# Recurrent attention and routed experts on one core: two products moved to GpSimd, the first expert's weights staged in two buffers, the slot table read through another queue

## The chip, the cores and the metric

The kernel runs on one core of a Trainium2 chip. The metric is device microseconds (us) of that core for one execution, lower is better. Engines are PE (TensorE), DVE (VectorE), ACT (ScalarE), POOL (GpSimd) and SP (SyncE, which here only issues DMAs); PEld is PE's loading of weights.

## What is computed

Two stages, the second fed by the first. The first is a recurrence over 768 steps for 4 x 8 heads of width 40; its output, laid out as 3072 tokens of 320 numbers, goes to one of 8 experts each:

```python
for t in range(S):                                   # 768 steps, state [4, 8, 40, 40]
    y[:, :, t] = einsum('bhd,bhde->bhe', rt, state)
    Sa = einsum('bhde,bhe->bhd', state, at)
    state = state * wt[:, :, None, :] - einsum('bhd,bhe->bhde', Sa, bt) + einsum('bhd,bhe->bhde', vt, kt)
x = y.transpose(0, 2, 1, 3).reshape(3072, 320)
logits = x @ w_gate                                  # 8 experts
e_idx = argmax(logits, axis=1)
gate_w = softmax(logits)[arange(N), e_idx]
eom = sigmoid(x @ w_output_gate)
for e in range(8):                                   # w1[e] 320 x 1024, w2[e] 1024 x 320
    mask = e_idx == e
    out[mask] = gate_w[mask, None] * eom[mask, e, None] * (maximum(x[mask] @ w1[e], 0) @ w2[e])
```

## The kernel before

**Attention.** The 768 steps are cut into 12 chunks `c` of 64. Within a chunk the recurrence becomes triangular systems, so that PE can work on it. Each chunk goes through four generators:

- `scan(c)` (L98) loads the decays `w` (L104) and `a`, `k`, `b` as one tile `D` (L106) through SP, and makes the running products `P` and `I` on DVE (L111 to L118).
- `prep(c)` (L126) makes what only the inputs need. `Av` is `a` times `I` and `a` times `P`, one product for columns 0 to 32 (L173) and one for 33 to 63 (L174), both on DVE. SP copies pieces of `Av` into `Am` (L180) and into `LA` (L167). DVE makes `KBt` (L190). PE multiplies `KBt` by `Am` (L203), ACT copies the result into `N` (L214) and `LA` (L216), and GpSimd zeroes the triangle of `LA` (an affine select, L218). GpSimd also clears parts of `LA` and `N` (L136, L144).
- `tinv` (L227) inverts the small triangles of two chunks at a time by products and sums on DVE (L290 and L295 are among them).
- `crit(c, q)` and `tail(c, q)` solve and finish a chunk in two units, q = 0 and 1, eight heads on each half of the partitions. `crit` applies `Tc` and `N` on PE (L368) with ACT's copies `As` between (L359, three in a unit); each copy waits for PE and PE for each copy. GpSimd's product `Dt` (L385) scales the state for the next chunk. `tail` transposes (L430), makes `M` (PE L440, DVE L444), `pY` (L455, L456), and DVE writes the result `x` (L458).

For each unit `route` stores `x` to a DRAM tensor `xd` (SP, L616), transposes it (L619) and computes the gate's logits (L623). After chunks 3, 7, 10 and 11, `pick` (L633) gives each token a slot of its expert, and GpSimd scatters 128 records of 16 bytes at a time into the table `tab` in DRAM (L695): eight scatters after chunk 3, eight after chunk 7, six and two after the last ones.

**Experts.** Each takes the tokens of its slots in groups of 120 columns times up to four. Weights are split into a high part (ACT cast) and the rest (DVE subtract), and each product is made of three (L776, L789 to L791), so PE runs nearly full there.

**What overlaps.** `run` (L473) steps through the units. At each step of `crit` it advances a background generator by four steps (`RATE`): preparation and inversion of later chunks, and, when the last of these is done, `early` (L809). That one stages the weights of expert 0 (`weights`, L708) in six blocks: SP load (L719, L722 or L729), ACT cast (L723, L730), DVE subtract (L725, L731), all through one buffer `st` (pool `sp0`, one buffer). Then, when the tokens of the first eight chunks have slots (`HALF`, L609) and 30 more steps are gone, `slots` (L798) reads the table into `tr` on SP (L802) and makes the index tiles on DVE (L804, L806). `tokens` (L734) gathers two groups of rows from `xd` on GpSimd (L745) and transposes them (L753), and the first four products of expert 0 follow (L776).

Each engine executes its own list in order. The lists are made by the tile framework's scheduler, which orders what the program issues by dependences and its own estimates; `issue_after(mark)` holds an instruction behind another one in the order. `mark['x']` is the last load of `XS` (L338), `mark['y']` the last `pY` product (L456). A tile's load can't begin before the last reader of the same buffer is done.

The lines that set where the weights and the table come:

```python
        with s.tc.tile_pool(name="sp0", bufs=1, side="right") as sp:
            w = s.weights(0, s.wpa, sp)
            s.W0 = next(w)
            yield from w
...
        for _ in range(30):
            yield
        with s.tc.issue_after(mark['x']):
            s.tabs = s.slots(s.tp0)
```

Of the kernel before, what the change touches and what calls it, by code (L numbers as in the profile page):

```python
# [9 lines left out]
F32 = mybir.dt.float32  # L10
# [4 lines left out]
AF = mybir.ActivationFunctionType  # L15
# [39 lines left out]
class Att:  # L55
# [70 lines left out]
    def prep(s, c):  # L126
# [45 lines left out]
        with s.tc.issue_after(s.mark['r', 0]) if c == 1 else ExitStack():  # L172
            V.tensor_tensor(out=Av[:, :, 0:33], in0=a[:, :, 0:33], in1=I[:, :, 1, ::-1], op=ALU.mult)  # L173
            V.tensor_tensor(out=Av[:, :, 33:64], in0=a[:, :, 33:64], in1=P[:, :, 0, 1:32], op=ALU.mult)  # L174
        with s.tc.issue_after(s.mark['n', 0]) if c == 1 else ExitStack():
# [167 lines left out]
    def crit(s, c, q):  # L343
# [13 lines left out]
        def move(h):  # L357
            x = s.p2.tile([128, 8, 40], F32, name="As", tag="As", bufs=2)
            nc.scalar.activation(out=x, in_=pa, func=AF.Copy, scale=s.hq[:, h:h + 1])  # L359
            return x  # L360
# [57 lines left out]
    def tail(s, c, q, sink):  # L418
# [38 lines left out]
        x = s.p2.tile([128, 8, 40], F32, name="x", bufs=2)  # L457
        nc.vector.tensor_tensor(out=x, in0=pY[:, :, 0:40], in1=WT[:, 8 * q:8 * q + 8], op=ALU.mult)  # L458
        s.post.append(sink(c, q, x))
# [98 lines left out]
class Moe:  # L558
# [148 lines left out]

    def weights(s, e, wp, sp):  # L708

        nc = s.nc  # L710
        w1h = wp.tile([128, 3, FF], F32R, name="w1h", tag="w1h")
        w1l = wp.tile([128, 2, FF], F32R, name="w1l", tag="w1l")
        w2h = wp.tile([128, 8, DM], F32R, name="w2h", tag="w2h")
        w2l = wp.tile([128, 8, DM], F32R, name="w2l", tag="w2l")
        yield w1h, w1l, w2h, w2l
        for k in range(3):
            st = sp.tile([128, FF], F32, name="st", tag="st")
            if k < 2:
                nc.sync.dma_start(out=st, in_=s.w1[e, 128 * k:128 * k + 128])  # L719
            else:  # L720
                for h in range(2):
                    nc.sync.dma_start(out=st[64 * h:64 * h + 64], in_=s.w1[e, 256:320])  # L722
            nc.scalar.copy(out=w1h[:, k], in_=st)  # L723
            l, r = (w1l[:, k], slice(0, 128)) if k < 2 else (w1h[64:128, 2], slice(64, 128))
            nc.vector.tensor_tensor(out=l, in0=st[r], in1=w1h[r, k].bitcast(F32), op=ALU.subtract)  # L725
            yield
        for k, n in ((0, 3), (3, 3), (6, 2)):
            st = sp.tile([128, FF], F32, name="st", tag="st")[:, 0:n * DM].rearrange("p (k f) -> p k f", k=n)
            nc.sync.dma_start(out=st, in_=s.w2[e, 128 * k:128 * (k + n)].rearrange("(k p) f -> p k f", p=128))  # L729
            nc.scalar.copy(out=w2h[:, k:k + n], in_=st)  # L730
            nc.vector.tensor_tensor(out=w2l[:, k:k + n], in0=st, in1=w2h[:, k:k + n].bitcast(F32), op=ALU.subtract)  # L731
            yield

# [63 lines left out]

    def slots(s, pool):  # L798

        nc = s.nc  # L800
        tr = pool.tile([TS, 32, 4], F32, name="tr", tag="tr")
        nc.sync.dma_start(out=tr, in_=s.tab.rearrange("(t p) f -> p t f", p=TS))  # L802
        tb = pool.tile([TS, 4, 32], F32, name="tb", tag="tb")
# [5 lines left out]
    def early(s, ctx, psx, mark):  # L809

        pool = lambda n, b: ctx.enter_context(s.tc.tile_pool(name=n, bufs=b, side="right"))
        s.wpa, s.tp0 = pool("wpa", 1), pool("tp0", 1)
        with s.tc.tile_pool(name="sp0", bufs=1, side="right") as sp:
            w = s.weights(0, s.wpa, sp)
            s.W0 = next(w)
            yield from w
        while not s.half:
            yield
        for _ in range(30):
            yield  # L820
        with s.tc.issue_after(mark['x']):
            s.tabs = s.slots(s.tp0)
        t = s.tokens(s.tabs, 0, 0, 2, s.tp0, psx)
# [242 lines left out]
```

## Time and profile before

| | |
|---|---|
| three runs | 726.17, 728.7, 730.5 us; median 728.7 |
| profiled execution | 729.31 us |
| span of its profile | 727.6 us |
| mean granted clock of PE | 0.947 of full |
| PE busy | 650.8 us (89% of the span), 8898 matmuls |
| PEld busy | 581.6 us (80%) |
| DVE busy | 470.3 us (65%) |
| ACT busy | 339.2 us (47%) |
| POOL busy | 206.5 us (28%) |
| DMA | 85.12 MB, mean 117 GB/s |

The span runs from the first to the last record of the execution that the profiler took. Some 1.7 us lie around it. Busy times of engines overlap. A "group" of the profile is all instructions of one line, engine and tile names, with their count, busy time and mean; behind it stands how long the engine was idle just before them, and what ended that. A row of the timeline has start and duration in us, engine, line, operation, output and inputs, shape, count, and in brackets an idle time of the engine ahead of it with what ended it ("<-DVE As L381"). The last `x` of attention is made at 467.6 us. The experts' products fill PE from 473 us to the end.

### The profile page before, as it was taken

The numbers are of one execution on the slowest core, as the hardware profiler recorded it, in microseconds if no ns is written. First come the engines' busy times: TensorE is split into PE (matmuls) and PEld (weight loads), VectorE is DVE, ScalarE is ACT, GpSimd is POOL, SyncE is SP. The second block draws the span as 40 slices with busy tenths as digits, with TensorE's granted clock in tenths as the row PEclk, the third lists the DMA queues.
The fourth block names the chain that finished last, engine by engine and source line by source line (L and its number), as shares of the span: only waits on it lengthen the run. The fifth ranks groups of instructions, "written<-read, shape, count | busy, mean of one in ns | idle before, by whom it ended". The sixth has DMA issues, their size and how long they took to land.

```text
span 727.6 us, 21192 instructions
## 1 busy us (share of the span) xinstructions
PE 650.8 (89%) x8898; PEld 581.6 (80%) x8898; DVE 470.3 (65%) x914; ACT 339.2 (47%) x781; POOL 206.5 (28%) x316
## 2 busy tenths in 40 slices
PE   6768997898999899899998699779999999999994
PEld 5556876787987788788887588679999998898994
DVE  6678689868986899897796254353575445554230
ACT  2567662674377368437632244142464334433120
POOL 8442220340233247222122100325533231402111
PEclk9867898999999999999999799999999999999998
DMA  7864653266337637632234551075475533431000
GB/s 165 190 150 128 155 143 79 76 152 160 99 111 180 133 79 178 156 92 86 76 76 88 115 141 50 20 184 174 114 240 147 166 117 104 153 109 34 18 13 28
DMA packets 64387, 85.12 MB, mean 117 GB/s; under 512 B 34586, under 2 KB 51613, under 8 KB 62846
## 3 DMA queue, kind: packets, MB, share of 16 engines
q1 hardware_dynamic: 60446, 74.79, 40.4%
q0 software_dynamic: 3840, 8.91, 4.3%
q8 instruction: 72, 1.18, 0.7%
q14 instruction: 29, 0.24, 0.1%
HBM read 67.59 MB, written 8.96 MB: 105 GB/s over the span
## 4 chain that ended last, share of the span: by engine, by line
PE 59%; DVE 12%; DMA 12%; ACT 7%; issue 5%; POOL 2%; SPq 1%; POOLq 0%; ACTq 0%; DVEq 0%
PE ph L776 14%; PE pa L368 5%; PE po L791 5%; DMA D<-in_din_dram 5%; PE po L789 5%; PE po L790 5%; PE pM L440 4%; DMA st<-in_w_dram 4%; PE pt L152 3%; PE pl L203 3%; PE pS L406 3%; PE pY L456 2%; ACT N L214 2%; PE pY L455 2%; PE pa L355 2%
## 5 line engine op out<-in xcount | busy, mean ns | idle before, releaser
L218 POOL TENSOR_SCALAR_AFFINE_SELECT LA<-LA 64x192 f32<-64x192 f32 x144 | 60.7, 451 | 85.9 <-ACT LA L216 79.4
L781 DVE SCALAR_TENSOR_TENSOR hl<-ph,hh 128x480 fp32r<-128x480 f32 (+1 forms) x76 | 41.8, 562 | 66.4 <-ACT hh L780 60.3
L789 PE MATMUL po<-w2h,hh 128*120 128x320 f32 x256 | 79.2, 313 | 3.6 <-ACT hh L780 3.5
L776 PE MATMUL ph<-xh,w1h 128*128 128x480 f32 (+1 forms) x228 | 79.4, 353 | 2.0 <-DVE hl L781 1.3
L776 PE MATMUL ph<-xl,w1h 128*128 128x480 f32 (+1 forms) x228 | 78.8, 348 | 0.0
L790 PE MATMUL po<-w2l,hh 128*120 128x320 f32 x256 | 78.0, 308 | 0.0
L780 ACT ACTIVATE hh<-ph 128x480 fp32r<-128x480 f32 (+1 forms) x76 | 36.8, 497 | 87.1 <-PE ph L776 79.9
L791 PE MATMUL po<-w2h,hl 128*120 128x320 f32 x256 | 75.8, 310 | 0.0
L794 POOL DMA_INDIRECT out_dram<-y,ti x32 | 33.5, 1047 | 137.5 <-DVE y L793 78.1
L359 ACT ACTIVATE As<-pa,hq 128x320 f32<-128x320 f32 x80 | 42.0, 527 | 55.7 <-PE pa L368 46.8
L203 PE MATMUL pl<-Am,KBt 120*128 120x192 f32 (+1 forms) x288 | 59.1, 337 | 9.5 <-ACT LA L216 6.0
L368 PE MATMUL pa<-As,Tc 64*32 64x40 f32 x1792 | 52.9, 208 | 16.0 <-ACT As L359 13.0
L214 ACT ACTIVATE N<-pl 32x192 f32<-32x192 f32 (+1 forms) x138 | 51.6, 374 | 25.8 <-PE pl L203 12.0
L368 PEld LDWEIGHTS pa<-As,Tc 64*32 64x32 f32 x1792 | 41.8, 114 | 26.9 <-ACT As L359 14.6
L456 PE MATMUL pY<-KB,M 128*64 128x64 f32 (+1 forms) x768 | 54.7, 230 | 7.0 <-DVE M L444 6.9
L695 POOL DMA_INDIRECT tab<-rec,si x24 | 24.8, 1033 | 114.5 <-DVE rec L692 47.8
L203 PEld LDWEIGHTS pl<-Am,KBt 120*128 120x128 f32 x288 | 44.6, 197 | 14.9 <-ACT LA L216 8.9
L456 PEld LDWEIGHTS pY<-KB,M 128*64 128x64 f32 x768 | 48.3, 143 | 9.8 <-DVE M L444 7.6
L455 PE MATMUL pY<-Sd,R 128*64 128x64 f32 (+1 forms) x704 | 55.7, 233 | 0.3 <-DVE base L669 0.3
L776 PE MATMUL ph<-xh,w1l 128*128 128x480 f32 (+1 forms) x152 | 52.9, 348 | 0.0
L440 PE MATMUL pM<-R,VU 128*128 128x128 f32 x384 | 51.0, 283 | 1.5 <-ACT VU L432 1.4
L789 PEld LDWEIGHTS po<-w2h,hh 128*120 128x120 f32 x256 | 46.3, 182 | 5.8 <-ACT hh L780 4.6
(186 smaller groups left out, 1564.5 us busy)
## 6 DMA issues: line engine op xcount, KB each, us to landing
D<-in_din_dram SPq DMA_DIRECT2D x12, 1080.0 KB
st<-in_w_dram SPq DMA_DIRECT2D x16, 512.0 KB
st<-in_w_dram SPq DMA_DIRECT2D x16, 480.0 KB
XS<-in_vt_dram SPq DMA_DIRECT2D x24, 256.0 KB
XU<-in_vt_dram SPq DMA_DIRECT2D x24, 256.0 KB
VU<-in_vl_dram SPq DMA_DIRECT2D x24, 208.0 KB
w<-in_win_dram SPq DMA_DIRECT2D x12, 371.2 KB
st<-in_w_dram SPq DMA_DIRECT2D x16, 256.0 KB
```

The source lines that it names most:

```text
L203: nc.tensor.matmul(pl[:, i, 0:nj], KBt[:, 6 * side + g0 + i].rearrange("p n t -> p (n t)"), Am[:, g0 + i:g0 + i + 6 * nj - 5:6, 0:64], sta ...
L214: s.mark['n', c] = nc.scalar.activation(out=nn, in_=pn, func=AF.Copy, scale=-1.0).ins
L218: g.affine_select(out=la[:, :, i], in_=la[:, :, i], pattern=[[0, nj], [1, C]], base=0, channel_multiplier=-1, compare_op=ALU.is_gt, fill=0.0)
L359: nc.scalar.activation(out=x, in_=pa, func=AF.Copy, scale=s.hq[:, h:h + 1])
L368: nc.tensor.matmul(pa[o + w:o + w + 32, i], m(p)[o:o + 64], x[o:o + 64, i, :], start=start, stop=True, tile_position=(o, o + w), skip_grou ...
L440: nc.tensor.matmul(pM[:, i], VU[:, h0 + i].rearrange("p n t -> p (n t)"), R[:, :, h0 + i], start=True, stop=True)
L455: nc.tensor.matmul(o, R[:, side, i, :], Sf[:, 40 * i:40 * i + w], start=True, stop=False)
L456: s.mark['y'] = nc.tensor.matmul(o, Ms[i // 4][:, i % 4, side, :], Kf[:, k:k + w], start=not c, stop=True).ins
L776: nc.tensor.matmul(ph, l, r, start=(i == 0), stop=(i == 7))
L789: nc.tensor.matmul(po, hh[f][:, ts_], w2h[:, f], start=(f == 0), stop=False)
L790: nc.tensor.matmul(po, hh[f][:, ts_], w2l[:, f], start=False, stop=False)
L791: nc.tensor.matmul(po, hl[f][:, ts_], w2h[:, f], start=False, stop=(f == 7))
```

## The change

1. From chunk 2 on, the two products of `Av` are issued on GpSimd (`g`) and no longer on DVE. Chunks 0 and 1 stay on DVE.
2. `weights` gets a second form, used for expert 0 only (`lag` 12). Pool `sp0` has two buffers. There are eight steps: step k issues the load of block k and the cast and subtract of block k - 2, with 12 yields behind each step. All of a step is ordered behind the last load of `XS` (`mark['x']`), the last `As` copy (`mark['as']`) and the last `x` (`mark['ds']`) that the program has issued by then.
3. `slots` reads the table through GpSimd's queue (now line 826), behind `mark['ds']` in place of `mark['x']`.

Lines below 716 keep their numbers. In the new kernel the weight loads are L720, L723 and L727, the casts L732 and L737, the subtracts L734 and L738, the gathers L769, the transposes of gathered rows L777, the first products L800.

```diff
         with s.tc.issue_after(s.mark['r', 0]) if c == 1 else ExitStack():
-            V.tensor_tensor(out=Av[:, :, 0:33], in0=a[:, :, 0:33], in1=I[:, :, 1, ::-1], op=ALU.mult)
-            V.tensor_tensor(out=Av[:, :, 33:64], in0=a[:, :, 33:64], in1=P[:, :, 0, 1:32], op=ALU.mult)
+            (g if c > 1 else V).tensor_tensor(out=Av[:, :, 0:33], in0=a[:, :, 0:33], in1=I[:, :, 1, ::-1], op=ALU.mult)
+            (g if c > 1 else V).tensor_tensor(out=Av[:, :, 33:64], in0=a[:, :, 33:64], in1=P[:, :, 0, 1:32], op=ALU.mult)
...
-            nc.scalar.activation(out=x, in_=pa, func=AF.Copy, scale=s.hq[:, h:h + 1])
+            s.mark['as'] = nc.scalar.activation(out=x, in_=pa, func=AF.Copy, scale=s.hq[:, h:h + 1]).ins
...
-        nc.vector.tensor_tensor(out=x, in0=pY[:, :, 0:40], in1=WT[:, 8 * q:8 * q + 8], op=ALU.mult)
+        s.mark['ds'] = nc.vector.tensor_tensor(out=x, in0=pY[:, :, 0:40], in1=WT[:, 8 * q:8 * q + 8], op=ALU.mult).ins
...
-    def weights(s, e, wp, sp):
+    def weights(s, e, wp, sp, lag=0, mark=None):
...
+        def load(k):
             st = sp.tile([128, FF], F32, name="st", tag="st")
...
+            return st
+
+        def halve(k, st):
+            if k < 3:
+                nc.scalar.copy(out=w1h[:, k], in_=st)
...
+        if not lag:
+            for k in range(6):
+                halve(k, load(k))
+                yield
+            return
+        st = {}
+        for k in range(6 + 2):
+            with ExitStack() as order:
+                for m in ('x', 'as', 'ds'):
+                    if m in mark:
+                        order.enter_context(s.tc.issue_after(mark[m]))
+                if k >= 2:
+                    halve(k - 2, st[k - 2])
+                if k < 6:
+                    st[k] = load(k)
+            for _ in range(lag):
+                yield
...
-    def slots(s, pool):
+    def slots(s, pool, q=None):
...
-        nc.sync.dma_start(out=tr, in_=s.tab.rearrange("(t p) f -> p t f", p=TS))
+        (q or nc.sync).dma_start(out=tr, in_=s.tab.rearrange("(t p) f -> p t f", p=TS))
...
-        with s.tc.tile_pool(name="sp0", bufs=1, side="right") as sp:
-            w = s.weights(0, s.wpa, sp)
+        with s.tc.tile_pool(name="sp0", bufs=2, side="right") as sp:
+            w = s.weights(0, s.wpa, sp, 12, mark)
...
-        with s.tc.issue_after(mark['x']):
-            s.tabs = s.slots(s.tp0)
+        with s.tc.issue_after(mark['ds']):
+            s.tabs = s.slots(s.tp0, s.nc.gpsimd)
```

The scheduler makes all lists anew, so rows move beyond the edited lines. Three places follow; numbers behind a tile's name tell its buffers apart.

DVE before, near the end of the preparations (chunk 11). `tmpf` and `Yt` belong to the inversion, `M` to a unit that is being finished, `rbm` is a test of the range of the decays:

```order
L411 TENSOR_TENSOR XS_155<-tmS,Dt 40x8x40
L118 TENSOR_TENSOR I<-I,rq 120x792
L174 TENSOR_TENSOR Av<-D,P 120x12x31
L466 TENSOR_REDUCE rbm<-wsq 120x1
L295 TENSOR_REDUCE Yt<-tmpf 128x8x4 x2
L467 TENSOR_REDUCE rbm<-rqm 120x1
L444 TENSOR_TENSOR M<-pM,mM 128x512
L173 TENSOR_TENSOR Av<-D,I 120x12x33
```

and GpSimd after the change, the last two chunks prepared (10 and 11):

```order
L385 TENSOR_TENSOR Dt<-LA 40x32
L218 AFFINE_SELECT LA<-LA 64x3x64 x2
L174 TENSOR_TENSOR Av<-D,P 120x12x31
L218 AFFINE_SELECT LA<-LA 64x3x64 x2
L173 TENSOR_TENSOR Av<-D,I 120x12x33
L218 AFFINE_SELECT LA<-LA 64x2x64 x2
L218 AFFINE_SELECT LA<-LA 64x3x64 x4
L218 AFFINE_SELECT LA<-LA 64x2x64 x2
L136 MEMSET LA 32x2112
L174 TENSOR_TENSOR Av<-D,P 120x12x31
L173 TENSOR_TENSOR Av<-D,I 120x12x33
```

The products left DVE's list, where they stood among pieces of the inversion and of `M`. On GpSimd those of chunk 10 stand between the selects of chunk 9, and those of chunk 11 behind the clearing of `LA`.

SP's queue where the weights and the table are read, before (units of chunks 9 and 10; `R`, `VU`, `XU`, `XS` are inputs of the units to come):

```order
L334 DMA VU_140<-in_vl_dram 104x8x64
L719 DMA st<-in_w_dram 128x1024
L802 DMA tr<-tab 120x32x4
L333 DMA R_139<-in_rl_dram 40x512 x2
L616 DMA xd<-x 128x320
L339 DMA XU_152<-in_vt_dram 64x1024
L338 DMA XS_155<-in_vt_dram 64x1024
L719 DMA st<-in_w_dram 128x1024
L334 DMA VU_144<-in_vl_dram 104x8x64
L722 DMA st<-in_w_dram 64x1024 x2
```

and after:

```order
L334 DMA VU_140<-in_vl_dram 104x8x64
L338 DMA XS_155<-in_vt_dram 64x1024
L333 DMA R_139<-in_rl_dram 40x512 x2
L616 DMA xd<-x 128x320
L720 DMA st<-in_w_dram 128x1024 x2
L339 DMA XU_152<-in_vt_dram 64x1024
L334 DMA VU_144<-in_vl_dram 104x8x64
L723 DMA st<-in_w_dram 64x1024 x2
L727 DMA st<-in_w_dram 128x3x320
```

The table read is gone from SP. The first two weight loads stand together behind the store of `x` of the first unit of chunk 9; before, the first stood ahead of that store and the second three transfers behind it.

ACT at the same place, before:

```order
L399 COPY XU_152<-pa 64x8x40
L723 CAST w1h<-st 128x1024
L359 ACTIVATE As<-pa,hq 128x320
L621 COPY xT<-pxt 128x384
L434 ACTIVATE Sd<-ptS 128x320
L432 COPY VU_144<-ptU 128x8x64
L624 COPY LG<-pxt 128x16
L359 ACTIVATE As<-pa,hq 128x320
L723 CAST w1h<-st 128x1024
L359 ACTIVATE As<-pa,hq 128x320
```

and after, with the scatters and the table read on GpSimd under it:

```order
L624 COPY LG<-pxt 128x16
L359 ACTIVATE As<-pa,hq 128x320
L732 CAST w1h<-st 128x1024 x2
L359 ACTIVATE As<-pa,hq 128x320
L398 COPY XU_156<-pa 64x8x40
L399 COPY XU_156<-pa 64x8x40
L732 CAST w1h<-st 128x1024
```

```order
L695 DMA tab<-rec,si 3840x4 x4
L385 TENSOR_TENSOR Dt<-LA 40x32
L695 DMA tab<-rec,si 3840x4 x4
L826 DMA tr<-tab 120x32x4
L769 DMA xg<-xd,ti 120x320 x2
L695 DMA tab<-rec,si 3840x4 x7
```

The first two casts stood ahead of the first and of the third `As` of a unit; now both stand together ahead of the third. On GpSimd the read follows the eight scatters that it depends on, with four of them ahead of `Dt` (two before the change).

## Rows read from the trace of the kernel before

**Rows 1.** By stretch: length, busy PE, PEld, DVE, ACT, POOL, clock, DMA share, GB/s.
```profile
45.00:365.00 320.00, 292.30 (x5390) 252.66 (x5391) 262.56 (x533) 194.44 (x495) 92.59 (x174) 0.95 0.50 124
395.00:435.00 40.00, 29.57 (x566) 26.00 (x562) 13.40 (x22) 12.92 (x25) 4.18 (x4) 0.83 0.55 128
```

**Rows 2.** Groups by line, the `Av` products: busy, mean ns | idle before, releasers.
```profile
L173 DVE TENSOR_TENSOR Av<-D,I 120x396 f32<-120x396 f32 x12 | 6.8, 568 | 6.6 <-DMA w<-in_win_dram 4.4 <-DMA xd<-x 2.0
L174 DVE TENSOR_TENSOR Av<-D,P 120x372 f32<-120x372 f32 x12 | 6.5, 546 | 13.0 <-DMA D<-in_din_dram 9.9 <-DMA VU<-in_vl_dram 1.7 <-DMA R<-in_rl_dram 1.4
```

**Rows 3.** Timeline of DVE, one wait for `D` in chunk 11.
```profile
307.63 0.55 DVE L174 TENSOR_TENSOR Av<-D,P 120x372 f32<-120x372 f32 x1 [2.61 <-DMA D<-in_din_dram]
```

**Rows 4.** Timeline of PE, five gaps that end with a DVE result.
```profile
54.70 1.01 PE L368 MATMUL pa<-As,Tc 64*32 64x40 f32 x24 [2.03 <-DVE As L381]
...
112.09 0.69 PE L619 MATMUL pxt<-ident,x 128*128 128x128 f32 x2 [1.33 <-DVE w L103]
...
178.88 0.55 PE L619 MATMUL pxt<-ident,x 128*128 128x128 f32 x3 [1.83 <-DVE x L458]
...
245.45 0.27 PE L456 MATMUL pY<-KB,M 128*64 128x64 f32 x1 [0.80 <-DVE M L444]
...
309.50 0.37 PE L456 MATMUL pY<-KB,M 128*64 128x64 f32 x1 [2.99 <-DVE M L444]
```

**Rows 5.** Busy time in the half-clock stretches behind those gaps: one, and the sum.
```profile
309.10:312.50 3.40, 3.00 (x60) 2.90 (x60) 3.40 (x12) 0.00 (x0) 0.00 (x0) 0.50 0.08 25
...
sum 20.50, PE 17.61 PEld 15.65 DVE 18.07 ACT 6.97 POOL 1.25; mean PE 4.40 PEld 3.91 DVE 4.52 ACT 1.74 POOL 0.31
```

**Rows 6.** GpSimd's selects (min/median/max ns) and timeline rows of three engines.
```profile
L218 POOL TENSOR_SCALAR_AFFINE_SELECT LA<-LA x144: 292/355/4680, 27.3 to 353.4; 64x192 f32<-64x192 f32 x96, 64x128 f32<-64x128 f32 x48
...
273.83 8.97 POOL L218 TENSOR_SCALAR_AFFINE_SELECT LA<-LA 64x192 f32<-64x192 f32 x8 [1.86 <-ACT As L359]
...
333.86 0.68 DVE L290 TENSOR_TENSOR tmpf<-Tt,Yt 128x512 f32<-128x512 f32 x1
...
335.06 0.83 DVE L290 TENSOR_TENSOR tmpf<-Tt,Yt 128x512 f32<-128x512 f32 x1
...
225.94 0.54 DVE L174 TENSOR_TENSOR Av<-D,P 120x372 f32<-120x372 f32 x1
...
233.79 1.41 PE L203 MATMUL pl<-Am,KBt 120*128 120x192 f32 x7 [0.43 <-ACT WT L154]
```

**Rows 7.** Timeline of SP's queue: the table read and the second weight load.
```profile
402.34 0.36 SPq L802 DMA_DIRECT2D tr<-tab  x1
...
407.32 0.53 SPq L719 DMA_DIRECT2D st<-in_w_dram  x1
```

**Rows 8.** Timeline of ACT and PE around those loads.
```profile
414.04 1.04 ACT L723 CAST w1h<-st 128x1024 fp32r<-128x1024 f32 x1 [10.26 <-DMA st<-in_w_dram]
...
400.65 0.55 PE L368 MATMUL pa<-As,Tc 64*32 64x40 f32 x20 [3.48 <-ACT As L359]
...
415.57 1.28 PE L368 MATMUL pa<-As,Tc 64*32 64x40 f32 x32 [6.30 <-ACT As L359]
```

**Rows 9.** Half-clock stretches from 401.3 (3.4 us) and 411.5 (10.3 us), summed.
```profile
sum 13.70, PE 9.63 PEld 8.58 DVE 3.12 ACT 4.42 POOL 0.00; mean PE 4.81 PEld 4.29 DVE 1.56 ACT 2.21 POOL 0.00
```

**Rows 10.** Timeline: two results `x`; two weight loads issued together, the second one's cast.
```profile
386.04 0.49 DVE L458 TENSOR_TENSOR x<-pY,WT 128x320 f32<-128x320 f32 x1 [0.60 <-PE pS L406]
...
395.40 0.49 DVE L458 TENSOR_TENSOR x<-pY,WT 128x320 f32<-128x320 f32 x1 [1.51 <-PE pY L456]
...
474.49 0.81 SPq L719 DMA_DIRECT2D st<-in_w_dram  x2
...
482.77 1.04 ACT L723 CAST w1h<-st 128x1024 fp32r<-128x1024 f32 x1 [1.81 <-DMA st<-in_w_dram]
```

**Rows 11.** The scatters as a group; the table read in the chain of waits.
```profile
L695 POOL DMA_INDIRECT tab<-rec,si x24 | 24.8, 1033 | 114.5 <-DVE rec L692 47.8 <-DMA tab<-rec,si 43.1 <-DVE M L444 20.1
...
402.34 4.26 DMA tr<-tab
```

More of the change, by code (lines that the diff above doesn't have):

```diff
@@ L715, in weights @@
         yield w1h, w1l, w2h, w2l
-        for k in range(3):
+        def load(k):
             st = sp.tile([128, FF], F32, name="st", tag="st")
@@ L719, in weights @@
                 nc.sync.dma_start(out=st, in_=s.w1[e, 128 * k:128 * k + 128])
-            else:
+            elif k == 2:
                 for h in range(2):
                     nc.sync.dma_start(out=st[64 * h:64 * h + 64], in_=s.w1[e, 256:320])
[L723 to L732, printed above, removed]
+            else:
+                k, n = ((0, 3), (3, 3), (6, 2))[k - 3]
+                st = st[:, 0:n * DM].rearrange("p (k f) -> p k f", k=n)
+                nc.sync.dma_start(out=st, in_=s.w2[e, 128 * k:128 * (k + n)].rearrange("(k p) f -> p k f", p=128))
@@ new lines, in load @@
+            return st
+        def halve(k, st):
+            if k < 3:
+                nc.scalar.copy(out=w1h[:, k], in_=st)
+                l, r = (w1l[:, k], slice(0, 128)) if k < 2 else (w1h[64:128, 2], slice(64, 128))
+                nc.vector.tensor_tensor(out=l, in0=st[r], in1=w1h[r, k].bitcast(F32), op=ALU.subtract)
+            else:
+                k, n = ((0, 3), (3, 3), (6, 2))[k - 3]
+                nc.scalar.copy(out=w2h[:, k:k + n], in_=st)
+                nc.vector.tensor_tensor(out=w2l[:, k:k + n], in0=st, in1=w2h[:, k:k + n].bitcast(F32), op=ALU.subtract)
```

## The prediction, made before the changed kernel ran

> **What bounds the kernel now.** I read the busy time by stretch first [rows 1], to see which engine is full where. From 45 to 365 us, where chunks are prepared while earlier chunks are solved, PE is busy 292.3 of 320 us and DVE 262.6: two nearly full engines that feed each other. From 395 to 435 us PE has only 29.6 us of work in 40, and a granted clock of 0.83. These are the two places that the change touches.
>
> For the first place the groups by line show the two products that make `Av` [rows 2]: 12 each, 568 and 546 ns, and before them 6.6 and 13.0 us in which DVE stood still, mostly for the load of `D`. The timeline of DVE shows one such wait [rows 3]: 2.61 us ahead of the product of chunk 11. DVE works in order, so whatever PE needs from it next comes late. PE's timeline has five gaps that end with a DVE result shortly after such a wait [rows 4]: 2.03, 1.33, 1.83, 0.80 and 2.99 us, 8.98 in all. Four of the five are followed by stretches in which the granted clock is half (1.2 GHz in place of 2.4). These last 20.5 us, and PE is busy 17.61 of them [rows 5]; at full clock that work would take half, so they cost up to 8.8 us.
>
> For the second place I read SP, ACT and PE together [rows 7, 8]. SP's queue issues the read of the slot table at 402.34 us, when the last scatter has landed. Everything behind it waits, the second weight load too, which goes out at 407.32. ACT has that load's cast in its order ahead of an `As` copy, waits 10.26 us for the data, and PE waits 6.30 us for the copy. The first load did the same a little earlier, for 3.48 us of PE. Two half-clock stretches follow, with 9.63 us of PE work in them [rows 9].
>
> **The change, part by part.** *The products move.* Ten chunks (2 to 11) take 10 x (0.568 + 0.546) = 11.1 us of work and most of the 19.6 us of waiting [rows 2] off DVE. I count the 11.1 us as nothing in themselves: PE is the fuller engine, and what it waits for DVE is in the gaps. Of the 8.98 us of gaps I take three quarters, 6.7, because some would wait for the next thing (the `M` product, an `As` copy); of the clock, two thirds of 8.8, 5.9. Bounds: 0, where the waits only change their name, and all of both.
>
> The waits for `D` now stand in GpSimd's queue. Behind them are the selects on `LA` of the chunk before, the clearing of `LA`, and `Dt`; a chunk prepared here is solved two chunks later, so 4 us are covered. `Av` itself may come later: in chunk 8 it ends at 226.5 and PE's first product with it starts at 233.79 [rows 6], 7.3 us later, with the copies into `Am` between. SP's queue has the copies of `Av` too, with loads of the next units behind them; a delay of 1 or 2 us is covered by their buffers (three of `XS` and `XU`).
>
> What does a product cost on GpSimd? No row has one. From below: DVE's own 0.55 us [rows 2]. From above: 4.7 us, since a select of 192 columns, 355 ns at the median, took 4680 ns in the worst case and eight of them 8.97 us [rows 6], in a stretch where DVE ran the scans and the `KBt` products. So GpSimd stands still while DVE reads two tiles in SBUF. I take 1.0 us, near the lower end, since the median select shows little delay. The other direction counts more: a DVE product that started behind a select took 0.83 us, and the same form 0.68 a little earlier [rows 6], so DVE waits some 0.15 us for a GpSimd read of 192 columns. For 20 products of twice the columns and two inputs I take 0.35 us each (0.15 to 0.9), 7 us of DVE, a third of it seen by PE: 2.3 us, bounds 0 and 6. The Trainium skill (GPSIMD Engine Reference, section Engine selection) speaks against this move: it wants products of two tiles on VectorE, as GpSimd is about half as fast. The select's 4680 ns agrees with its word on contention; no row shows the half speed. By that rule alone the step would be a loss; by the rows the waits that leave DVE weigh more than the product's length.
>
> *The weights.* Two buffers in place of one, casts two steps behind their loads. The new SP order puts the first two loads behind the `xd` store of unit (9,0), whose `x` is made at 395.40 [rows 10]. With a few issues between, they go out at about 396.6, and 512 KB each. In the later block of six, issued from 474.49, the cast of the second begins 8.3 us after [rows 10]. So the second cast ends near 396.6 + 8.3 + 1.0 = 405.9 and the `As` copy behind both casts near 406.5. When does PE want it? It is the third `As` of unit (10,0). A unit takes 9.4 us (386.04 to 395.40 [rows 10]), and its third `As` falls at about the time of `x`; so near 405. I take a new PE wait of 2 us (0 to 4) there. The next casts stand ahead of a `VU` copy and of two more `As`, each load again waiting for the subtract two steps before; 1.5 us more (0 to 4). Against that stand the 9.78 us of [rows 8] that go. Net 6.3 us, bounds 1.8 and 9.8. Of the clock, half of 9.63 is 4.8; a wait of 2 us may again bring 3.4 us at half (as the row of 309.1 in [rows 5]), 1.7, so 3.1 net.
>
> *The slot table on GpSimd's queue.* SP no longer stands until 402.34. GpSimd has nothing else to do then but the gathers that need the table anyway. `Dt` of chunk 10 now stands behind four scatters in place of two; it is wanted in the unit (10,0), after all eight. Nothing for both. The first products of expert 0 come later in PE's order, into the last unit; nothing either way.
>
> *The new order.* The order of all engines is made anew, and such an order has gaps of its own. I charge one like that of chunk 11: 2.99 us and half of 3.4 us of clock, 4.7.
>
> **Sum**, against the profiled 729.31 us: 6.7 + 5.9 - 2.3 + 6.3 + 3.1 - 4.7 = 15.0, so 714.3. The median of the three runs is 0.6 us lower than that execution: 714. A measurement of this kernel can tell 0.5%, 3.6 us, from no change.
>
> **Rivals.** *GpSimd gives it back* (0.14): `Av` and DVE's products block each other, and the first place gains nothing. What remains is 6.3 + 3.1 - 4.7 = 4.7: 724. For it speaks the 8.97 us of eight selects; against it that the waits, not the work, made the gaps.
>
> *The weight wait only moves* (0.10): the loads share their bandwidth, PE waits for the two casts together as long as before, and only the first place gains, 10.3 - 4.7 = 5.6: 723. For it: they go out later than the first load does now; against: the second one 11 us earlier.
>
> *The table read is slow* (0.10, the other side). SP's read of 3840 records of 16 bytes takes 4.26 us [rows 11]. On GpSimd a scatter of 128 records takes 1.03 us of the engine [rows 11]. If it pays by the record, 30 times as many take 31 us, until 433; with some 8 us for landing, index casts and two gathers (an estimate from the two rows) the rows of `x` are there at 441. PE has the transposes of these rows in its order right behind the `pY` of unit (10,1), three units after 395.4, at about 423. Its wait of 18 us and 7 us at half clock (3.5) against the sum's 15.0 give 729.3 + 6.5, or 736 us. It decides once the read takes more than about 15 us. Against it: the engine's time for an indirect DMA need not grow with its records, so most of the 1.03 us may be fixed. The Trainium skill (DMA: Bandwidth & Descriptors, section SWDGE vs HWDGE vs iDMA) says that GpSimd's processors compute these descriptors in software; elsewhere on that page many are said to be cheap. No row here shows it.
>
> *Nothing is gained* (0.06): PE is so nearly full that other waits fill the gaps: 728.
>
> **How the numbers follow.** The forecast has 0.60; its own range is 703 (all gaps and clock of the first place, no charge for the new order) to 721. Adding the rivals up to no change gives 703 to 727, which leaves out the slow table read and a little on either side. Faster by over 0.5% (below 725): 0.60 and nearly all of the first two rivals, 0.80; within: 0.10; slower: 0.10.
>
> **What would show it.** Right: no wait for `D` ahead of DVE products up to 365 us, PE idle below 20 us there; `L826` on GpSimd short, SP without a stop near 394 to 402; PE's waits for `As` between 395 and 425 below 4 us; the last unit of attention some 15 us earlier. Wrong: DVE's two-input products longer in the mean, PE waiting at the transposes of line 777, or new waits ahead of line 203.

## The result and the profile after

| | before | changed |
|---|---|---|
| median (lowest to highest) | 727.43 us (725.84 to 730.5, 4 runs) | 704.99 us (701.93 to 708.35, 4 runs) |
| profiled execution, span | 729.31 us, 727.6 us | 701.93 us, 700.2 us |
| last `x` of attention | 467.6 us | 442.0 us |

The ratio is 0.9688, interval 0.9621 to 0.9754: 22.4 us faster, where 15 were forecast. The profiled execution is the fastest of the four, and that of the kernel before lies above its median: the two profiles differ by 27.4 us, 5 more than the medians. A second set of six runs on another chip had a median of 705.12 us, ratio 0.9692 (0.9647 to 0.9736); its profile (span 702.5 us) is used below as "the second profile". Two of the ten executions of `wait_on_dve_no_work` below (731.7 and 733.1 us) were in a slower state and are left out of its median, its range and its ratio.

The page of the changed kernel, span and busy times:

```profile
span 700.2 us, 21203 instructions
PE 638.5 (91%) x8898; PEld 571.9 (82%) x8898; DVE 464.8 (66%) x894; ACT 338.1 (48%) x781; POOL 230.1 (33%) x337
```

PE does the same 8898 products in 638.5 us in place of 650.8. So 12.3 of the 27.4 us between the two spans are PE's own work done at a higher granted clock (a mean of 0.963 in place of 0.947), and 15.1 us are idle time that went. In the second profile PE is busy 641.2 us: 9.6 us less work time and 15.5 us less idle time. The idle time is the steady part, the clock is not. To see where, I cut both spans at the `x` of the units (1,1), (8,1) and (11,1). Busy time by stretch, before (length, PE, PEld, DVE, ACT, POOL, clock, DMA share, GB/s):

```profile
0.00:157.15 157.15, 126.43 (x1921) 108.03 (x1921) 122.81 (x230) 87.06 (x221) 55.51 (x122) 0.87 0.59 138
157.15:386.04 228.89, 217.50 (x4159) 190.43 (x4159) 192.92 (x413) 129.98 (x330) 67.91 (x119) 0.99 0.47 118
386.04:467.65 81.61, 67.51 (x1345) 60.02 (x1343) 34.27 (x71) 28.24 (x64) 10.09 (x10) 0.92 0.38 88
467.65:727.60 259.95, 239.37 (x1481) 223.11 (x1481) 120.33 (x202) 93.95 (x167) 72.97 (x66) 0.97 0.39 113
```

and after:

```profile
0.00:149.37 149.37, 122.09 (x1925) 104.66 (x1927) 120.48 (x221) 86.24 (x221) 63.96 (x130) 0.90 0.61 145
149.37:368.74 219.37, 210.90 (x4076) 184.31 (x4075) 183.50 (x392) 127.99 (x328) 78.92 (x130) 1.00 0.48 122
368.74:441.98 73.24, 66.17 (x1429) 59.73 (x1424) 40.21 (x82) 29.56 (x66) 13.26 (x13) 0.95 0.41 102
441.98:700.20 258.22, 239.37 (x1481) 223.17 (x1481) 120.63 (x202) 94.28 (x167) 73.91 (x66) 0.97 0.40 113
```

The first two stretches, where the `Av` products are made, give 7.8 and 9.5 us; the third, where the weights and the table come, 8.4; the experts 1.7. PE's idle time (length less busy) falls by 3.4, 2.9, 7.0 and 1.7 us. In the first stretches the rest is PE's busy time, 126.43 to 122.09 and 217.50 to 210.90 (79 products fewer stand in them; they come in the third stretch, which is shorter all the same).

Who held PE is in PE's waits (total, times, longest), after:

```profile
PE pS L406 <- DVE tmS L410: 7.5, 4, 5.7
PE pxt L619 <- DVE x L458: 7.2, 9, 1.7
PE ph L800 <- ACT xh L779: 4.1, 1, 4.1
PE pl L203 <- DMA Am<-Av: 3.4, 2, 1.7
PE pa L368 <- ACT As L359: 2.9, 6, 0.7
PE pY L456 <- DVE M L444: 0.8, 1, 0.8
```

and before, the waits that shrank:

```profile
PE pa L368 <- ACT As L359: 14.4, 10, 6.3
PE pY L456 <- DVE M L444: 6.9, 5, 3.0
PE pl L203 <- ACT LA L216: 6.0, 11, 1.9
```

All waits for `As` together, those behind the casts [rows 8] among them, went from 14.4 to 2.9 us, those for `M` (two of them in [rows 4]) from 6.9 to 0.8. Others grew: those for `x` from 4.3 to 7.2 us, those for the copies of `Av` into `Am` from 0.9 to 3.4, and those for `tmS` from 1.2 to 7.5, 5.7 of it in one piece. The timeline tells what that last one is (GpSimd, DVE, PE and ACT; then the half-clock stretch at this place, with the columns of the stretches above):

```profile
390.57 1.81 POOL L826 DMA_DIRECT2D tr<-tab  x1 [4.67 <-DVE w1l L734]
...
398.24 0.27 DVE L828 COPY tb<-tr 120x128 f32<-120x128 f32 x1 [6.30 <-DMA tr<-tab]
...
398.66 0.47 DVE L410 TENSOR_TENSOR tmS<-XS,pS 40x320 f32<-40x320 f32 x1
...
399.18 1.02 PE L406 MATMUL pS<-XU,KB 128*40 128x40 f32 x12 [5.72 <-DVE tmS L410]
...
393.56 1.04 ACT L732 CAST w1h<-st 128x1024 fp32r<-128x1024 f32 x1 [2.30 <-DMA st<-in_w_dram]
...
395.80:402.60 6.80, 3.42 (x38) 3.08 (x38) 4.16 (x8) 1.43 (x3) 2.57 (x2) 0.50 0.17 43
```

DVE has the copy of the table in its order ahead of `tmS`, waits 6.30 us for the read to land, and PE 5.72 us for `tmS`. The half clock begins inside this gap; PE is busy 3.42 us in it, so it costs up to 1.7 us. Before, the table stopped SP's queue [rows 7] and DVE too, but there `tmS` stood ahead of the copy, and PE lost next to nothing:

```profile
406.63 0.27 DVE L804 COPY tb<-tr 120x128 f32<-120x128 f32 x1 [4.89 <-DMA tr<-tab]
...
407.78 0.27 PE L456 MATMUL pY<-KB,M 128*64 128x64 f32 x1 [0.35 <-DVE M L444]
```

So it is not DVE's wait that is new, but what stands behind it.

The products themselves, as groups of GpSimd:

```profile
L174 POOL TENSOR_TENSOR Av<-D,P 120x372 f32<-120x372 f32 x10 | 10.2, 1019 | 66.3 <-DMA D<-in_din_dram 14.8 <-DMA VU<-in_vl_dram 12.1 <-DMA XS<-in_vt_dram 11.8
L173 POOL TENSOR_TENSOR Av<-D,I 120x396 f32<-120x396 f32 x10 | 10.1, 1011 | 4.6 <-DMA xd<-x 4.2
```

They take 1.0 us each, and it is now GpSimd that stands idle ahead of them, 70.9 us in all (it has less to do), where DVE stood 19.6 [rows 2].

### The profile page after: what moved, and what is told of

Read it like the earlier page. It is cut to its first block, busy times and chain, and to the rows that moved or that the text cites. A ratio compares the mean times of both kernels' runs of the same rounds, so it can differ in the third digit from the quotient of the medians.

```text
span 700.2 us, 21203 instructions
## 1 busy us (share of the span) xinstructions
PE 638.5 (91%) x8898; PEld 571.9 (82%) x8898; DVE 464.8 (66%) x894; ACT 338.1 (48%) x781; POOL 230.1 (33%) x337
## 5 line engine op out<-in xcount | busy, mean ns | idle before, releaser
L800 PE MATMUL ph<-xh,w1h 128*128 128x480 f32 (+1 forms) x228 | 79.8, 355 | 5.8 <-ACT xh L779 4.1
L800 PE MATMUL ph<-xl,w1h 128*128 128x480 f32 (+1 forms) x228 | 78.7, 349 | 0.0
L814 PE MATMUL po<-w2l,hh 128*120 128x320 f32 x256 | 77.8, 308 | 0.0
L203 PE MATMUL pl<-Am,KBt 120*128 120x192 f32 (+1 forms) x288 | 61.5, 347 | 6.8 <-DMA Am<-Av 3.4
L218 POOL TENSOR_SCALAR_AFFINE_SELECT LA<-LA 64x192 f32<-64x192 f32 x144 | 55.5, 419 | 33.7 <-ACT LA L216 32.2
L203 PEld LDWEIGHTS pl<-Am,KBt 120*128 120x128 f32 x288 | 46.1, 202 | 12.2 <-issue 5.7
L695 POOL DMA_INDIRECT tab<-rec,si x24 | 27.1, 1130 | 87.9 <-DMA tab<-rec,si 45.1
L455 PE MATMUL pY<-Sd,R 128*64 128x64 f32 (+1 forms) x704 | 53.8, 227 | 0.0
L800 PE MATMUL ph<-xh,w1l 128*128 128x480 f32 (+1 forms) x152 | 53.3, 351 | 0.0
L800 PEld LDWEIGHTS ph<-xh,w1h 128*128 128x128 f32 x228 | 44.2, 196 | 10.4 <-ACT xh L779 4.3
L769 POOL DMA_INDIRECT xg<-xd,ti x32 | 38.3, 1197 | 41.6 <-PE px L777 25.4
```

Source lines behind the costliest of these rows:

```text
L203: nc.tensor.matmul(pl[:, i, 0:nj], KBt[:, 6 * side + g0 + i].rearrange("p n t -> p (n t)"), Am[:, g0 + i:g0 + i + 6 * nj - 5:6, 0:64], sta ...
L218: g.affine_select(out=la[:, :, i], in_=la[:, :, i], pattern=[[0, nj], [1, C]], base=0, channel_multiplier=-1, compare_op=ALU.is_gt, fill=0.0)
L455: nc.tensor.matmul(o, R[:, side, i, :], Sf[:, 40 * i:40 * i + w], start=True, stop=False)
L800: nc.tensor.matmul(ph, l, r, start=(i == 0), stop=(i == 7))
L814: nc.tensor.matmul(po, hh[f][:, ts_], w2l[:, f], start=False, stop=False)
```

## The experiments

**The two parts apart.** `av_only`: the kernel before with the two `Av` lines of the diff and nothing else.

> Only the two products of Av go to GpSimd from chunk 2 on; weights and table read as before. Theory (the two parts gain in different stretches and add up): up to the x of unit (8,1) the new order of this part is the changed kernel's, so that x comes some 17 us earlier than in the kernel before, as it does in the changed kernel (368.7 against 386.0). The waits of PE for the As copies behind the weight casts (3.48 and 6.30 us before) stay. About 727.4 - 17 = 710 us, 706 to 714. Rival (the earlier units only wait longer for the last scatter, behind which SP's queue stands until the table is read): half of the 17 us is lost there, 717 to 721 us, and the waits for As grow by 5 us or more.

`weights_slots_only`: the changed kernel with

```diff
-            (g if c > 1 else V).tensor_tensor(out=Av[:, :, 0:33], in0=a[:, :, 0:33], in1=I[:, :, 1, ::-1], op=ALU.mult)
+            V.tensor_tensor(out=Av[:, :, 0:33], in0=a[:, :, 0:33], in1=I[:, :, 1, ::-1], op=ALU.mult)
```

and the same for columns 33 to 63.

> The Av products stay on DVE; weights in two buffers with later casts, and the table read on GpSimd. DVE, PE and ACT have the order of the kernel before up to chunk 9. Theory: x of unit (8,1) within 2 us of the kernel before (386.0), the gain lies behind it, 8 to 10 us by the last x (the changed kernel gained 8.4 us between those two), so about 718 us, 715 to 721. Rival (this part alone gains nothing, since the wait only moves from the casts to the table read, now on DVE, 6.3 us): 726 to 728 us.

Measured: `av_only` 711.7 us (708.6 to 715.6), ratio 0.9792 (0.9739 to 0.9845); `x` of (8,1) at 370.5 us. `weights_slots_only` 713.9 us (711.5 to 719.4), ratio 0.983 (0.9776 to 0.9884); `x` of (8,1) at 382.4, and from there to the last `x` 73.0 us where before needs 81.6. Each part is faster alone, the first in the first stretches (15.5 us by (8,1)), the second in the third (8.6 us). The rivals fall. Two misses: the second part's profile was also 3.6 us ahead at (8,1), with DVE's, ACT's and PE's order unchanged until chunk 9; PE's idle time up to there is 42.7 us, and 42.1 before, so no wait went, and this lead is PE's own work at a higher clock (4.2 us less busy time for 9 products fewer). And `av_only` gained 4.5 us in the third stretch too: PE's waits for `As` there fell from 11.0 to 5.8 us, where they were expected to stay. Its order is new, and no run tells what of it did that. The gains of the medians are 14.4 and 12.2 us and together 22.4, so some 4 us of them overlap.

**Wait or work?** The prediction rests on the claim that DVE's waits for `D` made PE's gaps and that its 11.1 us of work cost nothing. Two kernels take them apart. `work_on_dve_no_wait` gives DVE back as much work, without `D`, into a spare tile (for `c > 1`, as all the added lines below):

```diff
+            Ax = s.p1.tile([120, 12, 33], BF16, name="Ax")
+            V.tensor_tensor(out=Ax, in0=P[:, :, 1], in1=I[:, :, 1, ::-1], op=ALU.mult)
+            V.tensor_tensor(out=Ax[:, :, 0:31], in0=I[:, :, 0, 0:31], in1=P[:, :, 0, 1:32], op=ALU.mult)
```

> The changed kernel, and DVE makes 20 products of the same shapes as Av's (chunks 2 to 11) from P and I alone, into a spare tile that nobody reads: the work that left DVE comes back, without its wait for D. Theory (the waits made the gaps, the work costs nothing in itself): DVE busy up by 10 us, time 705 to 709 us. Rival (DVE is a bound in the first stretch, and its work is what left the path): 712 to 717 us, with the x of unit (8,1) 7 us or more later than in the changed kernel.

`wait_on_dve_no_work` gives it the wait, with copies of two columns:

```diff
+            Ax = s.p1.tile([120, 4], F32, name="Ax")
+            V.tensor_copy(out=Ax[:, 0:2], in_=a[:, 0, 0:2])
+            V.tensor_copy(out=Ax[:, 2:4], in_=a[:, 11, 62:64])
```

> The changed kernel, and DVE copies two columns of D twice in each of the chunks 2 to 11 into a spare tile: the wait for D comes back to DVE, with next to no work (20 copies of 120 x 2 numbers). Theory (the waits made the gaps): rows of DVE that wait for D 1 to 4 us again, PE gaps behind them, 710 to 717 us. Rival (the work was what counted, or the scheduler now puts the copies where D is there): 704 to 708 us.

Measured: the work 707.2 us (705.8 to 711.0), ratio 0.973 (0.9666 to 0.9795); the wait 726.5 us (720.4 to 731.1, 8 runs), ratio 0.9975 (0.9939 to 1.001). DVE's groups in the kernel with the work:

```profile
L174 DVE TENSOR_TENSOR Ax<-I,P 120x372 bf16<-120x372 f32 x10 | 6.1, 613 | 0.1
L173 DVE TENSOR_TENSOR Ax<-P,I 120x396 bf16<-120x396 f32 x10 | 5.7, 574 | 0.1
```

and in the kernel with the wait the copies, and the first two stretches:

```profile
L173 DVE COPY Ax<-D 120x2 f32<-120x2 f32 x10 | 1.7, 167 | 21.7 <-DMA D<-in_din_dram 21.7
L174 DVE COPY Ax<-D 120x2 f32<-120x2 f32 x10 | 1.6, 161 | 0.0
```

```profile
0.00:167.49 167.49, 130.86 (x2002) 112.80 (x2004) 125.18 (x236) 91.20 (x233) 69.74 (x141) 0.89 0.55 132
167.49:395.42 227.93, 212.59 (x4040) 186.58 (x4036) 185.89 (x402) 123.69 (x317) 76.76 (x118) 0.96 0.47 116
```

11.8 us of work cost 2.2 us, which is within the noise; the `x` of (8,1) came at 372.5 us, 3.7 and 2.1 us later than in the two profiles of the changed kernel, where the rival wanted 7 or more. 3.3 us of copies that wait 21.7 us cost 21.5, nearly all that the change had gained. PE's idle time up to `x` of (8,1) is 52.0 us with the wait (36.6 and 15.3) and 35.7 in the changed kernel. Two of the copies, and the gaps of PE behind them, in the kernel with the wait:

```profile
249.39 0.17 DVE L173 COPY Ax<-D 120x2 f32<-120x2 f32 x1 [2.98 <-DMA D<-in_din_dram]
...
254.22 0.37 PE L456 MATMUL pY<-KB,M 128*64 128x64 f32 x1 [2.77 <-DVE M L444]
...
298.09 0.17 DVE L173 COPY Ax<-D 120x2 f32<-120x2 f32 x1 [3.90 <-DMA D<-in_din_dram]
...
298.97 0.27 PE L456 MATMUL pY<-KB,M 128*64 128x64 f32 x1 [2.46 <-DVE M L444]
```

At 298.09 `M` is the next instruction of DVE behind the two copies, and PE waits for it. Eight gaps of PE of over 0.6 us, between 53 and 299 us, end with a DVE result less than 6 us behind such a wait, 16.5 us together; the excess of idle time over the changed kernel is 16.2. That is the claim shown, with two limits. DVE's order is made anew in both kernels. And the copies do not bring back the old state exactly: they wait 21.7 us for `D`, where the products stood 19.6 us before (9.9 of it put down to `D` by name, the rest to other transfers of SP [rows 2]), and PE's 52.0 us are more than the 42.1 of the kernel before (30.7 and 11.4). So the direction is shown, and not the size of each wait.

**What the products on GpSimd cost.** `av_on_dve_and_gpsimd` is `weights_slots_only` with a second set of the 20 products on GpSimd (from `D`, into the spare tile `Ax`); no order of another engine changes.

> The kernel weights_slots_only, and GpSimd makes the same 20 products (chunks 2 to 11) a second time into a spare tile (bfloat16 output) that nobody reads. DVE, ACT, PE and SP have the same order as there. So this is what GpSimd's work costs the others, with no wait of DVE taken away. Theory (small contention): 0 to 3 us slower than weights_slots_only, mean of DVE's two-input products up by under 0.05 us. Rival (GpSimd and DVE hold each other up, as the 8.97 us of eight selects could mean): 20 products of 1.0 us held and holding, 6 us or more slower, and products of 2 us or more on GpSimd.

`more_products_on_gpsimd` adds the same set to the changed kernel:

```diff
+            g.tensor_tensor(out=Ax, in0=a[:, :, 0:33], in1=I[:, :, 1, ::-1], op=ALU.mult)
+            g.tensor_tensor(out=Ax[:, :, 0:31], in0=a[:, :, 33:64], in1=P[:, :, 0, 1:32], op=ALU.mult)
```

> The changed kernel, and GpSimd makes the same 20 products a second time into a spare tile that nobody reads; DVE, ACT, PE and SP keep the order of the changed kernel. The earlier run with such a second set stood 14 us above its own base by the medians, 7.7 us by the profiles, but there DVE made the same products from the same tile at the same time. Theory (each product on GpSimd costs DVE 0.15 to 0.3 us, as the 3 to 6 us of more DVE time in the changed kernel say): DVE busy 3 to 6 us more than 464.8, time 707 to 711 us. Rival (20 products on GpSimd cost what that run showed, 8 to 14 us): 713 to 719 us.

Measured: the first 728.0 us (723.0 to 728.4), ratio 0.9998 (0.995 to 1.0045), 14.1 us above its base by the medians; the second 708.3 us (705.4 to 712.7), ratio 0.9744 (0.9673 to 0.9815), 3.3 us above. In the first, DVE's own `Av` products (their means were 568 and 561 ns in the base):

```profile
L173 DVE TENSOR_TENSOR Av<-D,I 120x396 f32<-120x396 f32 x12 | 10.3, 859 | 6.3 <-DMA w<-in_win_dram 4.4 <-DMA xd<-x 1.7
L174 DVE TENSOR_TENSOR Av<-D,P 120x372 f32<-120x372 f32 x12 | 7.3, 605 | 14.2 <-DMA D<-in_din_dram 6.6 <-DMA XS<-in_vt_dram 4.4 <-DMA VU<-in_vl_dram 1.7
```

In the second, the busy times:

```profile
PE 644.7 (91%) x8898; PEld 577.3 (82%) x8898; DVE 469.1 (66%) x894; ACT 338.1 (48%) x781; POOL 256.1 (36%) x357
```

The theory fell in the first run: it lost 14.1 us (7.7 between the profiles), as the rival's "6 us or more" wanted, and DVE was 9.3 us longer busy (479.8 for 470.5), 3.5 of it in the product of columns 0 to 32, beside which GpSimd made the same product from the same tile. The products on GpSimd took 1.1 us, not the 2 us of the rival. Where the rest of the loss comes from was not followed up. In the second run GpSimd's products stand beside other work of DVE: 4.3 us more of DVE than in the first profile of the changed kernel and 5.1 more than in the second (464.8 and 464.0), so 0.21 to 0.26 us of DVE for each product on GpSimd. The 3.3 us of time for 20 are within the noise of these runs.

**Chunk by chunk.** `av_from_chunk_6` is the changed kernel with `c > 5` in place of `c > 1`.

> The changed kernel, but the products of Av move only from chunk 6 on (12 of 20). In the runs with the changed kernel's order the x of unit (4,0) came 7 to 13 us earlier than before, and that of (8,1) 11 to 17 us. Theory (each wait for D taken off DVE brings its own part): of the gain up to (8,1) only 3 to 6 us are left, 712 to 717 us in all. Rival (one gap, or the new order as such, makes the gain): 704 to 708 us if it is one of the later ones.

Measured: 712.9 us (710.9 to 717.2), ratio 0.9819 (0.9756 to 0.9882). The total is the theory's, the way to it is not: `x` of (8,1) came 10.7 us earlier than before, where 3 to 6 were expected, so the later chunks bring more than half of the 15.7 to 17.3 us in the two profiles of the changed kernel. By PE's idle time up to there it is less than half: 39.3 us, between 42.1 before and 35.7 and 35.0. The gain at the start does come with the early ones: `x` of (1,1) is at 157.3 us here, as in the kernel before (157.2), and at 149.4 and 150.2 in the changed kernel. The third stretch then took 77.8 us, where the changed kernel takes 73.2 and 74.4:

```profile
375.39:453.16 77.77, 66.25 (x1406) 59.25 (x1401) 38.38 (x80) 29.55 (x66) 15.27 (x12) 0.93 0.40 96
```

PE stood idle 11.5 us of it. The order of DVE, ACT and PE is made anew here too; why it does worse there was not followed up.

**The table read.** `read_on_sp` is the changed kernel with `s.slots(s.tp0)`; only the read moves, back to SP.

> The changed kernel with the table read back on SP, behind the first two weight loads; all other engines keep their order. The read waits for the last scatter (landed at about 388.5 in the changed kernel), and SP's queue stands behind it from about 383 on; it takes 4.3 us in place of 7.7 us. Theory (the queue does not matter, the two buffers and the later casts do): DVE's wait for the table shrinks by some 3 us, the held loads are not wanted before 395, so 700 to 706 us against the changed kernel's 705.0. Rival (the other queue is what freed SP and made the gain): the transfers behind the read come late, PE waits 4 us or more for their users between 385 and 410, 709 to 713 us.

`index_on_gpsimd` leaves the read where the change put it, and GpSimd makes the index copies:

```diff
-        nc.vector.tensor_copy(out=tb, in_=tr.rearrange("p t f -> p f t"))
+        (q or nc.vector).tensor_copy(out=tb, in_=tr.rearrange("p t f -> p f t"))
-        nc.vector.tensor_copy(out=ti, in_=tb[:, 0:2])
+        (q or nc.vector).tensor_copy(out=ti, in_=tb[:, 0:2])
```

> The changed kernel, and the two index copies behind the table read (tb, ti) on GpSimd in place of DVE; nothing else in any engine's order differs. In the changed kernel DVE waits 6.30 us for the read to land, and PE 5.72 us for the tmS product behind it; 6.8 us at half clock follow. Theory (DVE's wait holds PE): DVE no longer waits there, PE's gap is ended by the As copy that came at 395.2 in the changed kernel, so it shrinks from 5.7 to about 1.7 us, and some of the half clock goes (0 to 3 us): 705.0 - 4 - 1.5 = 699.5 us, 697 to 702. Rival (the gathered rows bound, and they wait for the same read): 704 to 706 us, with a new wait of PE at the transposes of line 777.

Measured: 707.2 us (703.0 to 711.3), ratio 0.9713 (0.9638 to 0.9789), and 706.0 us (700.8 to 707.0), ratio 0.9696 (0.9648 to 0.9745). Neither can be told from the changed kernel. The first lies between its two forecasts, with a new wait of PE as its rival wanted; the second missed its theory (697 to 702) and came out at the time of its rival, but not by the wait at line 777 that this one named. With the read on SP, PE and ACT show:

```profile
404.74 0.74 PE L368 MATMUL pa<-As,Tc 64*32 64x40 f32 x16 [5.44 <-ACT As L359]
...
403.09 1.04 ACT L732 CAST w1h<-st 128x1024 fp32r<-128x1024 f32 x1 [6.73 <-DMA st<-in_w_dram]
```

With the index copies on GpSimd, PE:

```profile
398.21 1.01 PE L368 MATMUL pa<-As,Tc 64*32 64x40 f32 x24 [3.51 <-ACT As L359]
```

With SP, DVE no longer waits for the table, but the third weight load stands behind the read in SP's queue, goes out at 396.2 in place of 388.8, and PE has a gap of 5.44 us for the cast where it had 5.72 for the copy. With the copies on GpSimd the gap at `tmS` is gone; ahead of it PE waits 3.51 us for the first two casts (0.57 in the first profile of the changed kernel, 1.90 in the second). The third stretch takes 71.7 us there, against 73.2 and 74.4. So the read, the casts and `tmS` end within a few microseconds of each other, and what is taken from one is mostly given to the next; which queue the read uses is worth nothing that these runs can show.

**A version that might do better.** `index_gpsimd_late_w2` adds to the last one that the casts of expert 1's w2 stand behind those of its gathered rows, the last of which `s.xm` marks (PE's 4.07 us at line 800):

```diff
+        def late(w, t):
+            for _ in range(3):
+                yield next(w)
+            yield from t
+            for _ in range(3):
+                with tc.issue_after(s.xm):
+                    next(w)
+                yield
-        unit(0, 0, 2, chain(w, t))
+        unit(0, 0, 2, late(w, t))
```

> The changed kernel with the two index copies on GpSimd, and the casts of expert 1's w2 held behind the casts of its gathered rows (before, ACT had the three w2 casts first, and PE waited 4.07 us at line 800 for a row cast, with 6.8 us at half clock behind it). Theory (both are waits that end on PE): the 5.7 us gap behind the table's read shrinks by 4 us, that at line 800 by 3 us, some of the half clock goes (0 to 5 us): 705 - 7 - 2 = 696 us, 693 to 700. Rival (the w2 products or the gathered rows themselves wait next): PE waits 3 us or more at line 813 or at the transposes of line 777, 702 to 707 us.

Beside it ran the changed kernel again.

> The changed kernel once more, on the same chip as the run before, so that the two are compared directly. Expected from its first four runs (701.9 to 708.4 us): a median of 705 us, 702 to 708. The profile is expected to differ from the first by its half-clock stretches alone (the x of unit (8,1) between 368 and 375 us).

Measured: 704.9 us (703.3 to 706.8), ratio 0.9691 (0.9647 to 0.9736), beside 705.1 us (702.9 to 706.2): the same. The rival held. PE's waits in the experts of the new version (the first line in total, times, longest), where one of 3.31 us stood at line 800 in the second profile:

```profile
PE px L777 <- DMA xg<-xd,ti: 4.0, 4, 1.8
...
463.77 0.37 PE L777 MATMUL px<-ident,xg 120*64 120x120 f32 x2 [0.71 <-DVE xl L780]
467.36 0.60 PE L800 MATMUL ph<-xh,w1h 128*128 128x240 f32 x3 [1.53 <-ACT xh L782]
```

The third stretch is 3.1 us shorter (71.2 us for 74.4), the experts 1.6 us longer (259.4 for 257.8): the long wait became several short ones. No version was found that beats the changed kernel.

## Why the prediction was right

The forecast was 714 us, the range 703 to 727; measured 705.0. The direction and both places were right. The gain was half as large again, which puts the time near the low end of the range, and two steps came out otherwise than written.

- **The waits leave DVE** (6.7 us): right in kind. In the profile of the changed kernel no DVE instruction up to 365 us waits for `D`, and the two kernels of wait and work show that the wait counted. It was sized too small: PE's idle time fell by 6.3 us over the first two stretches (7.1 in the second profile), net of what the products on GpSimd cost, where 6.7 - 2.3 = 4.4 were forecast. From 45 to 365 us PE stood idle 27.7 us before and 20.1 and 20.7 in the two profiles after, just above the 20 that the prediction named as a sign. The reading of [rows 2] as "mostly for the load of `D`" has 9.9 of 19.6 us by name; the rest stands under other transfers of SP.
- **The clock there** (5.9 us): PE's busy time in these stretches fell by 10.9 us. 79 products fewer stand in them, 4.1 us at 52 ns of busy time for one (210.90 us / 4076), which leaves 6.8. Right for this profile, but by some luck, as it is not a fixed amount: see the last section.
- **A product on GpSimd** (1.0 us; DVE 0.35 us longer for each): 1.01 us and 0.21 to 0.26. The upper end, 4.7 us, drawn from the slowest select, was far off. The Trainium skill (GPSIMD Engine Reference, Engine selection) calls GpSimd about half as fast here, and the trace agrees: 1019 against 546 ns and 1011 against 568. By that rule alone the step would have been a loss; it was a gain, since little waits for these products. Not nothing: PE's waits for the copies of `Av` ahead of line 203 grew by 2.5 us, to 3.4, one of the signs that the prediction named for being wrong.
- **DVE's 11.1 us at nothing**: 11.8 us put back cost 2.2, within the noise. Right as far as these runs can tell.
- **The weights** (6.3 us net of 9.78): the two waits for casts [rows 8] shrank to 0.57 us in the first profile, 1.90 in the second. The 2 us expected at the third `As` is that; the further 1.5 us didn't come as waits for `As`. Not all of this is the second buffer's: with `av_only` too the waits for `As` fell there, from 11.0 to 5.8 us.
- **The table read at "Nothing for both"**: this is the step that failed. I looked at SP's queue and at GpSimd's, not at who uses the table. Its first user is DVE. In the new order `tmS` stands behind that user, before it stood ahead; so DVE's wait, 4.89 us then and 6.30 now, reaches PE only now. The read lands 7.7 us after its issue, where SP's took 4.26 [rows 11], and PE lost 5.72 us (5.04 in the second profile) and up to 1.7 us by the half clock from 395.8 to 402.6. The Trainium skill (DMA: Bandwidth & Descriptors, SWDGE vs HWDGE vs iDMA) has the descriptors of SP's queue made by hardware with a faster setup; these two numbers agree with it.
- **The new order** (4.7 us lost): no such gap came up in the first two stretches, where the new order rather gained. In the sum this charge stood in for the gap at the table, which is about as large; that is luck, not a reading.
- **The rivals.** The slow read was 1.81 us of GpSimd for 3840 records, not 31, far from the 15 us from which it would have decided; a scatter of 128 records takes 1.03 [rows 11], so 30 times the records did not cost 30 times the time. GpSimd giving it back fell too: 20 products on it cost DVE 4.3 to 5.1 us of busy time, and PE's idle time in the first two stretches fell by 6.3 us all the same. That the weight wait only moves is half true: of 9.8 us one gap of 5.7 is left under another name.
- **The experts**, forecast unchanged, gave 1.7 us in the one profile and 2.2 in the other, all of it PE's idle time; no run explains them.

In sum, 15.1 us of idle time and 12.3 of clock between the two profiles (15.5 and 9.6 with the second), where the terms make 7.7 and 7.3. The mechanism was right in both places; of the idle time that went, the terms had about half.

## What to carry to other kernels

An engine that works in order and feeds the bound engine should not be the one that waits for a load: ask of each of its instructions what it waits for and what stands behind it, and give the waiting one, even at twice the time, to an engine that nobody waits for. When a transfer changes queue, look past both queues to the first instruction that reads the tile, and to what is behind that one. The busy time that leaves a nearly full engine is a poor measure of the gain: here 11.8 us of it cost 2.2 when put back, while putting back the wait cost 21.5.

## What was not expected of the hardware

With one and the same order on DVE, ACT and PE, the half-clock stretches fall differently from one execution to the next. The first two stretches of `index_on_gpsimd`:

```profile
0.00:153.13 153.13, 125.93 (x1925) 107.88 (x1927) 119.83 (x220) 86.26 (x221) 62.55 (x130) 0.88 0.60 141
153.13:374.43 221.30, 213.03 (x4076) 186.27 (x4076) 181.76 (x392) 127.82 (x328) 81.25 (x130) 0.98 0.49 121
```

It makes the same 6001 products there as the first profile of the changed kernel, and PE is busy 5.97 us longer (338.96 for 332.99), at a mean granted clock of 0.88 and 0.98 for 0.90 and 1.00; the `x` of (8,1) came at 374.4 in place of 368.7. A difference of 5 us between two profiles of attention can be the clock alone; idle time of PE told the kernels apart better. Up to `x` of (8,1) it was 42.1 and 42.7 us in the two kernels whose DVE makes all the products, before and `weights_slots_only`, and 35.0 to 37.2 in the six profiles in which all 20 have moved and nothing was put back or added beside them.

Two engines that made the same product from the same tile at the same time paid more than two with different work: DVE was 0.47 us longer busy for each product of GpSimd (9.3 us for 20), and its own product of columns 0 to 32 took 859 ns in the mean, for 568; beside other work it was 0.21 to 0.26 us for each. Whether the tile or the time counts, no run separates.
